# Another hand-written order for the queues, PSUM banks and copy engines of a gated linear recurrence followed by a gated causal convolution block

## Chip, cores and metric

One Trainium2 chip, one of its cores. The metric is device time in microseconds; the kernel before takes 287.73 us (median of 3 runs, 287.46 to 287.93). Lower is better.

## The reference, cut to what matters

Four batches of 6336 positions with 256 channels, float32 in and out. First the recurrence:

```python
log_a = 8 * sigmoid(r_gate) * log(sigmoid(a_param))
a_t   = exp(log_a)
x_g   = sqrt(max(1 - a_t * a_t, 1e-6)) * sigmoid(i_gate) * x
h     = a_t[:, t] * h + x_g[:, t]          # over t, y[:, t] = h
```

Then the gated block on y: a causal depthwise convolution of 5 taps gives the gate, and

```python
out = (sigmoid(conv5(y)) * (y @ w_val)) @ w_out
```

## The kernel before, in words

The 25344 positions of the four batches lie one behind the other. They are cut into 51 **windows** (w = 0 to 50), 48 of them with 512 positions and 3 with 256, and the windows into 28 **chunks** (c = 0 to 27): chunks 3 to 25 have two windows (chunk c has windows 2c-3 and 2c-2), the others one. All arrays live in rings in SBUF, and PSUM is used as 8 banks. Every step is a short word, and one long string, ORDER (L38), lists all words in the order in which they are written to the engines' queues. Each engine takes its own words strictly in that order; nothing reorders them later. A word may name the PSUM banks that it writes, behind an @. Semaphores hold an engine at a word until what it reads is there and what it overwrites has been read.

The words, by engine:

- SyncE (SP) issues the DMAs: `lr`, `li`, `lx` load a window of r_gate, i_gate and x (L292), `st` stores a window of the output (L546). A load waits until the ring place, 4 windows deep, has been read.
- ScalarE (ACT): `ta` and `tb` are tanh of r and i of a chunk (L310, L313; sigmoid(v) is (1 + tanh(v/2)) / 2), `ex` the exp that gives a_t (L378), `rt` the square root for a batch of up to three chunks (L405), `tg` tanh of the convolution's gate of a window (L502), `ca` a copy of a finished window from PSUM to the output ring (L535), `sa` a square (L394). `rt` needs another table of functions than the rest, so a table load stands ahead of and behind each `rt` (L562).
- GpSimd (POOL): `sq` squares a_t (L386), `pp` adds 1 to tanh of i (L320), `up` multiplies by x (L332).
- VectorE (DVE): `uv` does the work of `pp` and `up` for windows 1, 2 and 6 (L346), `xg` multiplies by the norm (L450, L446 for the last two chunks), `sc` is the scan over a half of the channels (L483), `gv` gate times value (L515), `cd` the same copy as `ca` (L533).
- TensorE (PE): `tr`, `nt`, `xt` are transposes (L357, L420, L461, L435), `xp` a plain pass of x into PSUM (L337), `cv` the convolution as 20 small products with diagonal weights (L495), `vl` and `ou` the two products with w_val and w_out (L510, L525), `wm` five products whose result nobody reads (L364).

The path of the data: r goes through `ta`, `tr`, `ex`, `sq`, `rt`, `nt`; i and x through `tb`, `pp`, `up`; they meet in `xg`, then `xt`, `sc`, `cv`, `tg`, with `vl` into `gv`, `ou`, a copy, `st`. The twelve `rt` join all: `rt.b` needs the squares of all its chunks, and each chunk's `xg` waits for its `rt`. `rt.10` is that of chunks 23 to 25, `rt.11` of the last two. Each finished window needs one copy, by `cd` on VectorE or `ca` on ScalarE: that is the choice of copy engine.

The lines that run the list (L557):

```python
for word in ORDER.split():
    word, _, at = word.partition("@")
    name, *idx = word.split(".")
    if table.get(name, have) != have:
        have = table[name]
        nc.scalar.preload_act_table_set(have)
    emit[name](*[int(k) for k in idx], *[int(k) for k in at.split(",") if k])
```

Of the kernel before, what the change touches and what calls it, by code (L numbers as in the profile page):

```python
# [17 lines left out]
    [512, 512], [512, 512], [512, 512], [512, 512], [512, 512], [512, 512], [512, 512], [512, 512], [512, 512],  # L18
    [512, 512], [512, 512], [512, 512], [512, 512], [512, 512], [512, 512], [512, 512], [512], [256]]
BATCHES = [[0], [1], [2], [3, 4], [5, 6, 7], [8, 9, 10], [11, 12, 13], [14, 15, 16], [17, 18, 19], [20, 21, 22],  # L20
    [23, 24, 25], [26, 27]]
# [17 lines left out]
s_ident s_small s_kt s_diag lr.2 lr.0 s_wl.3 lr.1 li.0 lr.3 s_wl.2 ta.2 ta.0 lr.4 tr.0.1@0 tr.2.0@1 lr.6 ta.1 lr.5  # L39
tr.1.0@2 tb.0 tr.0.0@3 li.1 tr.2.1@4 ex.2.0 li.2 tr.1.1@5 li.3 ex.1.1 lx.0 ex.0.1 sq.1.1 li.4 ex.1.0 sq.2.0 ex.0.0  # L40
ex.2.1 sq.1.0 ta.3 sq.2.1 pp.0 sq.0.0 sq.0.1 ta.4 tb.1 lr.10 tr.3.0@4,5 tb.2 lr.9 lr.8 lr.7 lx.2 tr.3.1@2,3 ex.3.0
s_wl.1 up.0 lx.1 lx.4 wm.10@6 ex.3.1 sq.3.0 wm.5@6 lx.3 wm.3@6 tb.3 sq.3.1 wm.9@6 wm.6@6 ta.6 pp.4 sq.4.1 ta.5 lr.13
li.5 xp.2@2,3 li.6 sq.4.0 li.7 lr.14 tr.5.0@4,5 lx.6 uv.2 pp.3 rt.0 rt.2 nt.0@0 up.4 xg.0 rt.1 xt.0@0,1 xp.1@2 rt.3
sc.0.0 nt.1@3 up.3 lx.5 nt.2@0 uv.1 s_wl.0 xg.1 xg.2 xt.1@2,3 sc.0.1 lx.7 sc.1.0 nt.3@6,7 lr.12 sc.1.1 xg.3 ex.5.0
xt.2@0,1 sc.2.1 sc.2.0 tb.4 cv.0@2,3 tr.5.1@4,5 xt.3@6,7 lr.11 li.8 sq.5.0 ex.5.1 tg.0 sc.3.0 pp.5 sc.3.1 cv.2@0,1
s_wcast cv.1@4,5 ta.8 xp.6@2,3 uv.6 vl.0@6,7 tg.1 tg.2 vl.2@0,1 up.5 ta.7 sq.6.1 lx.8 li.9 li.10 lr.17 lr.18
nt.4@2,3 gv.0 tb.5 tr.7.0@6,7 ou.0.0@4 gv.2 ex.7.0 xg.4 sq.6.0 cd.0.0 tr.7.1@0,1 sq.5.1 vl.1@2,3 ou.2.0@4,5 ex.7.1
gv.1 xt.4@6,7 ou.1.0@2 lx.9 li.12 cv.4@0,1 cd.2.0 cv.3@4,5 pp.7 sq.7.1 tb.6 pp.8 sq.7.0 tg.4 tg.3 rt.4 sc.4.1 st.0
sc.4.0 li.11 lr.15 lr.16 st.2 up.7 pp.9 li.14 li.13 vl.3@0,1 vl.4@4,5 gv.3 gv.4 cd.1.0 ou.3.0@0,1 pp.10 up.8 sq.8.1
cd.3.0 cv.6@6,7 st.1 ou.4.0@2,3 wm.12@4 tg.6 cd.4.0 wm.1@4 nt.5@2,3 xg.5 lx.10 tb.7 st.3 vl.6@0,1 gv.6 ta.9 xt.5@2,3  # L50
ou.6.0@0,1 cv.5@6,7 nt.6@4,5 ta.10 up.9 sc.5.0 sc.5.1 lx.11 up.10 wm.0@2 tr.9.0@2,3 tg.5 st.4 lx.12 tb.8 vl.5@6,7
ex.9.0 xg.6 cd.6.0 xt.6@4,5 pp.11 sq.8.0 pp.12 tr.9.1@0,1 up.11 ex.9.1 li.16 li.15 lr.19 lr.20 gv.5 lr.22 st.6 lr.21
nt.7@6,7 cv.7@2,3 sc.6.1 up.12 ou.5.0@0,1 sc.6.0 sq.9.0 tg.7 tb.9 cv.8@2,3 cd.5.0 xg.7 lx.13 lx.14 li.18 ta.11
vl.7@4,5 cv.9@0,1 xt.7@6,7 gv.7 tr.11.1@4 tg.9 tg.8 ex.11.1 ta.12 ou.7.0@0,1 st.5 lx.15 lx.16 li.17 li.19 lr.26
lr.24 sc.7.1 sc.7.0 cv.10@2,3 vl.10@4,5 wm.7@7 vl.8@6,7 tg.10 sq.10.1 pp.13 pp.14 sq.10.0 cd.7.0 sq.9.1 pp.15 gv.10
rt.5 gv.8 st.7 lr.23 li.20 vl.9@2,3 up.13 up.14 tr.12.0@0 pp.16 ou.10.0@4,5 gv.9 ou.8.0@6,7 cd.8.0 ou.9.0@2,3
wm.16@1 nt.8@6,7 tr.11.0@1 cd.9.0 cd.10.0 tb.10 sq.11.1 up.16 xg.8 cv.11@4,5 lx.17 st.9 lr.25 xt.8@6,7 sc.8.1 tg.11
vl.11@2,3 wm.17@4 ex.12.0 tr.12.1@0 nt.9@4,5 gv.11 pp.17 up.15 pp.18 ex.11.0 ex.12.1 sq.12.1 sq.11.0 cv.12@2,3
sq.12.0 xg.9 ta.13 wm.13@7 ou.11.0@4,5 sc.8.0 xt.9@0,1 cd.11.0 cv.14@6,7 cv.13@4,5 tb.11 tg.12 ta.14 tg.14 tg.13
tr.13.0@2,3 tr.13.1@6,7 sc.9.0 ex.13.0 sc.9.1 up.17 st.10 li.21 vl.12@4,5 ex.13.1 nt.10@0,1 lx.18 li.22 gv.12 up.18  # L60
xg.10 lr.28 st.8 lr.27 tb.12 vl.13@2,3 st.11 ou.12.0@4,5 xt.10@0,1 cv.16@6,7 pp.20 pp.19 sq.13.1 gv.13 ou.13.0@2,3
lx.20 lx.21 lr.30 lx.19 ta.15 sq.13.0 pp.21 up.20 cd.12.0 cv.15@4,5 sc.10.1 sc.10.0 lr.29 li.23 tg.16 cd.13.0 li.24
lx.22 tg.15 vl.16@6,7 vl.14@4,5 gv.14 cv.18@0,1 vl.15@2,3 pp.22 rt.6 up.19 li.25 ou.14.0@4,5 gv.16 gv.15 cd.14.0
wm.14@6 ou.15.0@2,3 tg.18 lr.31 li.26 nt.11@4,5 sq.14.0 sq.14.1 up.21 up.22 vl.18@6,7 cd.15.0 xg.11 xt.11@4,5 tb.13
gv.18 cv.17@0,1 nt.12@6,7 ta.16 lr.32 lx.23 sc.11.1 lx.24 st.15 pp.23 pp.24 xg.12 st.13 li.27 li.28 vl.17@2,3
tr.15.1@6,7 sc.11.0 tg.17 tb.14 up.23 ou.16.0@0,1 cd.16.0 ex.15.1 ta.17 cv.19@4,5 lr.34 lr.33 tg.19 gv.17 xt.12@0,1
tr.15.0@6,7 st.14 lx.25 sc.12.0 sc.12.1 li.30 ou.17.0@2,3 pp.25 ex.15.0 ou.18.0@4,5 cv.20@6,7 up.24 tb.15 cd.17.0
cd.18.0 tg.20 cv.21@0,1 pp.26 sq.15.1 sq.16.1 nt.13@2,3 vl.19@6,7 tg.21 xg.13 st.12 lx.26 lx.28 st.17 lx.27 sq.15.0
li.29 st.16 li.31 lr.35 gv.19 vl.20@0,1 gv.20 xt.13@2,3 ou.20.0@0,1 sc.13.0 sq.16.0 vl.21@6,7 ou.19.0@4,5 gv.21
ta.18 cd.20.0 sc.13.1 ou.21.0@6,7 cv.22@0,1 lr.38 st.20 lr.36 rt.7 ca.19.0 li.32 lr.37 up.25 pp.27 up.26 pp.28 lx.29  # L70
nt.14@4,5 cd.21.0 xg.14 vl.22@2,3 tr.17.1@6,7 tg.22 tb.16 up.28 up.27 ex.17.1 nt.15@0,1 lx.30 gv.22 xg.15 xt.14@4,5
tr.17.0@2,3 cv.23@0,1 sc.14.0 sc.14.1 ex.17.0 pp.30 cv.24@6,7 pp.29 st.19 tg.23 vl.24@2,3 ou.22.0@0,1 tg.24 gv.24
vl.23@6,7 xt.15@4,5 ta.19 sq.18.1 sq.18.0 sq.17.0 sq.17.1 ou.24.0@2,3 tb.17 cd.22.0 gv.23 li.33 li.34 cv.26@0,1
up.29 cd.24.0 ou.23.0@6,7 st.18 ta.20 pp.32 ca.23.0 tg.26 cv.25@2,3 up.30 pp.31 sc.15.0 tg.25 li.35 tr.19.0@6,7
# [32 lines left out]
def kernel(  # L107
# [11 lines left out]
    nc = tc.nc  # L119
# [70 lines left out]
    with tc.manual_schedule():  # L190
# [403 lines left out]
```

## Time and profile before

| what | value |
|---|---|
| median of 3 runs | 287.73 us |
| span of the profiled execution, first to last instruction | 286.4 us |
| busy ScalarE (ACT) | 273.6 us, 96% |
| busy TensorE (PE) | 251.8 us, 88% |
| busy VectorE (DVE) | 246.8 us, 86% |
| busy GpSimd (POOL) | 241.6 us, 84% |
| moved by DMA | 104.76 MB, mean 366 GB/s |

The profiled execution has no time of its own beside its span; the median of the runs stands 1.33 us above that span, which is what lies around the first and the last instruction. Busy times are those of one execution. In the rows of the trace, a line begins with the start and the duration in us (or, in groups, ends with total, mean and idle time before), then engine, source line, operation and what it writes and reads; `[1.09 <-PE banks L525]` says that the engine stood idle for 1.09 us before and what released it.

### The profile page before, as it was taken

What the parts mean: (1) busy time and instruction counts of PE and PEld (TensorE: products, weight loads), DVE (VectorE), ACT (ScalarE), POOL (GpSimd) and SP (SyncE); (2) the same over time, 40 slices, a digit from 0 to 9 for tenths busy, and PEclk for the clock granted to TensorE, in tenths of its full rate; (3) what the DMA queues carried; (4) which work ended last, traced back from release to release, by engine and by line L of the source; (5) the groups of instructions that cost most, each with busy time, mean ns of one, the idle gap of its engine ahead of it and who ended that gap; (6) DMA issues with size and microseconds to landing.
All of it is one profiled execution on the core that took longest, in us unless ns stands there. A gap on an engine that the chain in (4) does not pass through costs nothing.

```text
span 286.4 us, 6382 instructions
## 1 busy us (share of the span) xinstructions
PE 251.8 (88%) x2552; PEld 171.1 (60%) x2576; DVE 246.8 (86%) x214; ACT 273.6 (96%) x198; POOL 241.6 (84%) x161
## 2 busy tenths in 40 slices
PE   1387778899999999988988999989989899999993
PEld 1253447456656767455756676656646774767562
DVE  4002898969999899999999999999999999999991
ACT  5999999999999999999999999999999999898984
POOL 1659589899999999999999999999996999874600
PEclk9999999999999999999999999999999999999999
DMA  7999999999999999999999999999999999994536
GB/s 243 384 373 407 409 403 408 388 366 376 410 408 366 418 367 392 414 410 334 405 364 413 411 332 356 420 416 419 415 401 333 359 416 406 364 356 170 192 150 256
DMA packets 29996, 104.76 MB, mean 366 GB/s; under 512 B 3335, under 2 KB 3854, under 8 KB 29966
## 3 DMA queue, kind: packets, MB, share of 16 engines
q1 hardware_dynamic: 29952, 104.35, 94.5%
q8 instruction: 20, 0.33, 0.5%
q14 instruction: 10, 0.08, 0.1%
q10 hardware_dynamic: 14, 0.01, 0.0%
HBM read 78.39 MB, written 25.95 MB: 364 GB/s over the span
## 4 chain that ended last, share of the span: by engine, by line
ACT 33%; PE 29%; DVE 14%; issue 12%; DMA 8%; SPq 1%; ACTq 0%; DVEq 0%
ACT ering L405 8%; PE banks L495 8%; DVE yring L483 7%; PE banks L525 7%; DMA rring<-in_r_gate_dram 6%; ACT tgring L502 6%; ACT taring L310 5%; ACT tbring L313 5%; ACT aring L378 5%; PE banks L510 5%; PE banks L461 3%; DVE tgring L515 3%; PE banks L420 3%; ACT L562 3%; DVE oring L533 2%
## 5 line engine op out<-in xcount | busy, mean ns | idle before, releaser
L386 POOL TENSOR_TENSOR ering<-aring 128x1024 f32<-128x1024 f32 (+2 forms) x54 | 91.5, 1714 | 16.7 <-ACT aring L378 16.4
L332 POOL TENSOR_TENSOR uring<-tbring,xring 128x1024 bf16<-128x1024 bf16 (+1 forms) x48 | 101.1, 2119 | 3.6 <-DMA xring<-in_x_dram 3.1
L483 DVE TENSOR_TENSOR_SCAN yring<-aring,yring,banks 128x1024 bf16<-128x1024 f32 (+5 forms) x50 | 101.7, 2064 | 2.1 <-PE banks L461 1.9
L495 PE MATMUL banks<-yring,diag 64*64 64x512 bf16 (+7 forms) x1080 | 62.1, 361 | 2.3 <-ACT aring L378 1.6
L515 DVE SCALAR_TENSOR_TENSOR tgring<-tgring,banks 128x1024 bf16<-128x1024 bf16 (+1 forms) x51 | 59.1, 1178 | 4.0 <-PE banks L510 3.4
L320 POOL TENSOR_SCALAR tbring<-tbring 128x1024 bf16<-128x1024 bf16 (+1 forms) x48 | 49.1, 1032 | 6.8 <-ACT tbring L313 6.7
L378 ACT ACTIVATE aring<-banks,khf 128x2048 f32<-128x2048 bf16 (+3 forms) x38 | 54.2, 1476 | 0.4 <-PE banks L357 0.3
L525 PE MATMUL banks<-wo,tgring 128*128 128x256 bf16 x396 | 51.0, 274 | 3.7 <-DVE tgring L515 3.2
L502 ACT ACTIVATE tgring<-banks 128x1024 bf16<-128x1024 f32 (+1 forms) x51 | 50.2, 1011 | 2.0 <-PE banks L495 1.9
L510 PE MATMUL banks<-yring,wv 128*128 128x512 bf16 (+4 forms) x192 | 48.1, 359 | 3.7 <-ACT tgring L502 1.9
L310 ACT ACTIVATE taring<-rring 128x2048 bf16<-128x2048 f32 (+2 forms) x28 | 47.9, 1718 | 1.4 <-DMA rring<-in_r_gate_dram 1.4
L525 PEld LDWEIGHTS <-tgring 128*128 128x128 bf16 x396 | 41.2, 114 | 13.1 <-DVE tgring L515 8.8
L313 ACT ACTIVATE tbring<-iring 128x2048 bf16<-128x2048 f32 (+2 forms) x28 | 48.2, 1726 | 0.0
L405 ACT ACTIVATE ering<-ering 128x4096 bf16<-128x4096 f32 (+5 forms) x16 | 44.8, 2840 | 0.1
L495 PEld LDWEIGHTS <-diag 64*64 64x64 bf16 x1080 | 29.0, 106 | 25.6 <-issue 9.9
L533 DVE COPY oring<-banks 128x1024 f32<-128x1024 f32 (+1 forms) x36 | 41.9, 1182 | 1.4 <-PE banks L525 0.7
L357 PE MATMUL banks<-ident_b,taring 128*128 128x128 bf16 x396 | 29.9, 230 | 9.4 <-ACT taring L310 6.7
L357 PEld LDWEIGHTS <-taring 128*128 128x128 bf16 x396 | 26.5, 103 | 14.2 <-ACT taring L310 7.4
L510 PEld LDWEIGHTS <-wv 128*128 128x128 bf16 x216 | 19.7, 98 | 24.5 <-issue 10.3
L450 DVE TENSOR_TENSOR uring<-banks,uring 128x2048 bf16<-128x2048 bf16 (+2 forms) x26 | 29.4, 1134 | 3.5 <-PE banks L420 3.2
L420 PE MATMUL banks<-ident,ering 128*128 128x128 f32 x192 | 28.3, 289 | 1.1 <-ACT ering L405 0.9
L461 PE MATMUL banks<-ident,uring 128*128 128x128 f32 x192 | 25.9, 276 | 3.5 <-DVE uring L450 2.8
(49 smaller groups left out, 154.0 us busy)
## 6 DMA issues: line engine op xcount, KB each, us to landing
rring<-in_r_gate_dram SPq DMA_DIRECT2D x48, 512.0 KB, 8.2
iring<-in_i_gate_dram SPq DMA_DIRECT2D x48, 512.0 KB, 8.7
xring<-in_x_dram SPq DMA_DIRECT2D x48, 512.0 KB, 8.2
out_dram<-oring SPq DMA_DIRECT2D x48, 512.0 KB, 6.5
rring<-in_r_gate_dram SPq DMA_DIRECT2D x3, 256.0 KB, 4.1
iring<-in_i_gate_dram SPq DMA_DIRECT2D x3, 256.0 KB, 6.5
xring<-in_x_dram SPq DMA_DIRECT2D x3, 256.0 KB, 8.5
out_dram<-oring SPq DMA_DIRECT2D x3, 256.0 KB, 5.2
```

The costliest lines, as they stand in the source:

```text
L310: nc.scalar.activation(**tangent(c, taring, NTR, rring, NRI))
L313: nc.scalar.activation(**tangent(c, tbring, NTI, iring, NII))
L332: nc.gpsimd.tensor_tensor(out=u, in0=t1, in1=xt, op=ALU.mult)
L378: nc.scalar.activation(out=dst, in_=src, func=ACT.Exp, scale=khf[:, h:h + 1], bias=khf[:, h:h + 1])
L386: nc.gpsimd.tensor_tensor(out=e, in0=a, in1=a, op=ALU.mult)
L405: nc.scalar.activation(out=ering[:].bitcast(BF16)[:, 4 * o:4 * o + 2 * n], in_=ering[:, 2 * o:2 * o + 2 * n], func=ACT.Sqrt, scale=-0.25, ...
L483: nc.vector.tensor_tensor_scan(out=yring[:, h, col:col + o1 - o0], data0=aring[:, h, a_at[c] + o0:a_at[c] + o1], data1=xT[:, o0:o1], initi ...
L495: nc.tensor.matmul(out=gp[oh * 64:oh * 64 + 64, h, a:b], lhsT=diag[half * 64:half * 64 + 64, h, k, :], rhs=yring[half * 64:half * 64 + 64, ...
L502: nc.scalar.activation(out=tgring[:, w % NTG, :, 0:wins[w]], in_=live.pop(("gp", w))[:, :, 0:wins[w]], func=ACT.Tanh, scale=0.5)
L510: nc.tensor.matmul(out=val[:, m, a:b], lhsT=wv[:, hk, m * P:(m + 1) * P], rhs=yring[:, hk, col:col + b - a], start=(hk == 0), stop=(hk == ...
L515: nc.vector.scalar_tensor_tensor(out=tgring[:, w % NTG, :, 0:wins[w]], in0=tgring[:, w % NTG, :, 0:wins[w]], scalar=1.0, in1=live.pop(("va ...
L525: nc.tensor.matmul(out=ops[:, j * D:(j + 1) * D], lhsT=gv[:, hk, j:wins[w]:J], rhs=wo[:, hk, :], start=(hk == 0), stop=(hk == H - 1))
```

## The change: what it does

ORDER is replaced as a whole by another list of the same length (976 words). The ring sizes, the chunks, the groups and the batches are the same. Beside the order, three things differ: the banks behind @ (among them two unequal banks for some `xt`, such as `xt.0@0,4`, and banks for the two set-up words, which had theirs in the code); which engine copies eight windows (16, 22, 24, 32 and 36 go from VectorE to ScalarE, 19, 23 and 39 from ScalarE to VectorE); and the places of the 17 `wm`. An unused function goes. Source lines behind it move up by one to five.

```diff
 ORDER = """
-s_ident s_small s_kt s_diag lr.2 lr.0 s_wl.3 lr.1 li.0 lr.3 s_wl.2 ta.2 ta.0 lr.4 tr.0.1@0 tr.2.0@1 lr.6 ta.1 lr.5
...
-s_wl.1 up.0 lx.1 lx.4 wm.10@6 ex.3.1 sq.3.0 wm.5@6 lx.3 wm.3@6 tb.3 sq.3.1 wm.9@6 wm.6@6 ta.6 pp.4 sq.4.1 ta.5 lr.13
...
+s_ident s_small s_kt@0 s_diag@1 lr.0 lr.1 lr.2 lr.3 ta.0 ta.1 tr.1.0@4 lr.4 tr.0.0@6 tr.0.1@7 lr.5 ta.2 ex.0.0 ex.0.1
...
+li.7 sc.0.0 xp.1@7 wm.5@5 sc.0.1 cv.0@4,5 tg.0 uv.1 xg.1 xt.1@1,7 sc.1.0 xt.2@0,6 sc.1.1 sc.2.1 lx.5 s_wcast lx.7 lx.8
+ex.5.0 nt.3@4,5 xg.3 tr.5.1@6,7 tb.4 sq.6.0 sq.5.0 sc.2.0 xt.3@2,3 sc.3.0 cv.1@4,5 li.9 li.10 ex.5.1 sq.6.1 pp.5
...
-        def s_kt():
-            kps = banks[:, 0]
+        def s_kt(at):
+            kps = banks[:, at]
...
-        def s_diag():
-            wps = banks[:, 1]
+        def s_diag(at):
+            wps = banks[:, at]
...
-        def op_sv(c, h):
-            e, a = squares(c, h)
-            nc.vector.tensor_tensor(out=e, in0=a, in1=a, op=ALU.mult)
```

What this makes of the queues, at three places. First ScalarE at the start of the program, behind the exp of the set-up. A row is a source line, an operation, what it writes and reads and its shape; 128x512 in taring is a window of 256 positions. Before:

```order
L237 ACTIVATE ktmp<-ktmp 128x2
L310 ACTIVATE taring<-rring 128x1024
L310 ACTIVATE taring<-rring 128x512 x2
L313 ACTIVATE tbring<-iring 128x512
L378 ACTIVATE aring<-banks,khf 128x512
L378 ACTIVATE aring<-banks,khf 128x256 x4
L378 ACTIVATE aring<-banks,khf 128x512
```

After the change:

```order
L236 ACTIVATE ktmp<-ktmp 128x2
L309 ACTIVATE taring<-rring 128x512 x2
L309 ACTIVATE taring<-rring 128x1024
L377 ACTIVATE aring<-banks,khf 128x256 x4
L309 ACTIVATE taring<-rring 128x2048
L377 ACTIVATE aring<-banks,khf 128x512
L309 ACTIVATE taring<-rring 128x2048
L377 ACTIVATE aring<-banks,khf 128x512
```

The two short windows come first, the tanh of i moves behind them, and the large tanh of r stand between the exps. Up to the first table load, which stands ahead of the first square roots, ScalarE has the same 19 words in both lists.

Second, ScalarE behind the square root of batch 6 (the row L405 or L400 over 128x6144). Before, down to the square root of batch 7:

```order
L405 ACTIVATE ering<-ering 128x6144
L562 ACT_TABLE_LOAD
L502 ACTIVATE tgring<-banks 128x1024
L313 ACTIVATE tbring<-iring 128x2048
L310 ACTIVATE taring<-rring 128x2048
L502 ACTIVATE tgring<-banks 128x1024
L313 ACTIVATE tbring<-iring 128x2048
L378 ACTIVATE aring<-banks,khf 128x2048
```

After the change:

```order
L400 ACTIVATE ering<-ering 128x6144
L557 ACT_TABLE_LOAD
L497 ACTIVATE tgring<-banks 128x1024
L312 ACTIVATE tbring<-iring 128x2048 x2
L530 COPY oring<-banks 128x1024
L497 ACTIVATE tgring<-banks 128x1024
L377 ACTIVATE aring<-banks,khf 128x2048 x2
L309 ACTIVATE taring<-rring 128x2048
```

A copy (that of window 16) stands between the tanh, where there was none. Ahead of `rt.10` ScalarE has 3 copies before (windows 19, 23, 33) and 6 after (16, 22, 24, 32, 33, 36); of all other kinds it has the same number ahead of `rt.10` in both lists.

Third, VectorE ahead of the product of chunk 23 (the next-to-last row, L450 or L445 over 128x2048), which is the first to need `rt.10`. Before:

```order
L515 SCALAR_TENSOR_TENSOR tgring<-tgring,banks 128x1024 x2
L533 COPY oring<-banks 128x1024
L515 SCALAR_TENSOR_TENSOR tgring<-tgring,banks 128x1024
L533 COPY oring<-banks 128x1024 x2
L450 TENSOR_TENSOR uring<-banks,uring 128x2048
L515 SCALAR_TENSOR_TENSOR tgring<-tgring,banks 128x1024 x2
```

After the change:

```order
L510 SCALAR_TENSOR_TENSOR tgring<-tgring,banks 128x1024 x3
L478 SCALAR_TENSOR_TENSOR yring<-aring,yring,banks 128x1024
L528 COPY oring<-banks 128x1024 x3
L445 TENSOR_TENSOR uring<-banks,uring 128x2048
L510 SCALAR_TENSOR_TENSOR tgring<-tgring,banks 128x1024 x2
```

The copy of window 39, which ScalarE had behind `rt.10`, stands here on VectorE ahead of it; the eight products that window 39 needs first (`ou.39`) moved ahead of `nt.23`, TensorE's first word behind `rt.10`. From `nt.23` to the end TensorE has 44 words before and 43 after, the same but for `ou.39`.

More of the change, by code (lines that the diff above doesn't have):

```diff
@@ L99 @@
[L99 to L102 removed]
+s_ident s_small s_kt@0 s_diag@1 lr.0 lr.1 lr.2 lr.3 ta.0 ta.1 tr.1.0@4 lr.4 tr.0.0@6 tr.0.1@7 lr.5 ta.2 ex.0.0 ex.0.1
+tr.1.1@0 ex.1.1 ex.1.0 lr.6 li.2 li.0 ta.3 tr.2.1@7 ex.2.1 tr.2.0@6 lx.0 lr.8 lr.7 ta.4 lr.9 lr.10 ex.2.0 tb.2 sq.1.1
@@ L103 @@
+ou.50.0@3 ca.50.0 st.50
 """
```

130 lines of the change are left out of this document (63 added, 67 removed).

## Prediction

> **What bounds the kernel now.** All numbers are of one profiled execution with a span of 286.4 us; the median of the runs, 287.73, lies 1.33 above it, and I add the difference that I work out to that median. First the busy time of the engines in six stretches, cut at ScalarE's first tanh, its first table load, the start and the end of `rt.10` and TensorE's last product. Columns: stretch, its length, busy time of PE, PEld, DVE, ACT and POOL (with counts), granted clock, DMA share, GB/s.
>
> ```profile
> 0.00:4.54 4.54, 0.23 (x1) 0.18 (x1) 0.88 (x6) 1.49 (x2) 0.97 (x7) 1.00 0.57 190
> 4.54:26.48 21.94, 12.88 (x77) 8.15 (x78) 2.92 (x15) 20.71 (x20) 13.70 (x13) 1.00 1.02 380
> 26.48:238.87 212.39, 196.25 (x2047) 134.37 (x2068) 202.64 (x161) 211.95 (x140) 203.75 (x127) 1.00 1.01 391
> 238.87:244.20 5.33, 5.17 (x60) 2.88 (x52) 5.22 (x6) 5.32 (x1) 5.33 (x4) 1.00 1.00 404
> 244.20:282.80 38.60, 37.30 (x377) 25.55 (x382) 35.11 (x29) 33.55 (x36) 17.84 (x13) 1.00 0.67 247
> 282.80:286.40 3.60, 0.00 (x0) 0.00 (x0) 0.00 (x0) 0.58 (x1) 0.00 (x0) 0.90 0.56 218
> ```
>
> The third row carries most: for 212.39 us ScalarE is busy 211.95 and idle 0.44. VectorE and POOL are near it (202.64, 203.75), so it has little to spare from others, but the one that never waits is ScalarE. **From 26.48 to `rt.10` the length is the sum of ScalarE's work.** In the fifth row this has changed: TensorE is busy 37.30 of 38.60. The chain that ended last, in order of time (start, length, what), confirms it:
>
> ```profile
> 238.87 5.34 ACT ering L405
> 244.25 1.24 PE banks L420 x8
> ...
> 249.42 0.87 PE banks L525 x8
> ...
> 281.43 0.70 DVE tgring L515
> 282.13 0.05 issue
> 282.17 0.63 PE banks L525 x4
> 282.82 0.58 ACT oring L535
> ```
>
> The square root of L405 ends at 244.21 and releases TensorE's transposes (`nt.23`); from there nearly all pieces down to 282.8 are TensorE's. So the end is: start of ScalarE, plus its work up to `rt.10`, plus TensorE's work from `nt.23` on, plus 3.60 for the last copy and store.
>
> **The change part by part.**
>
> (1) ScalarE's work ahead of `rt.10`. The order's rows show that only copies differ: 3 before, 6 after. What a copy costs in a full queue, from a copy and what starts behind it:
>
> ```profile
> 168.50 1.02 ACT L535 COPY oring<-banks 128x1024 f32<-128x1024 f32 x1
> 169.40 1.97 ACT L502 ACTIVATE tgring<-banks 128x1024 bf16<-128x1024 f32 x2
> ```
>
> From start to start 169.40 - 168.50 = 0.90 us. Three more are **+2.70 us**, with no cover, since ScalarE has no idle time there to lose. The other side is lighter by what VectorE no longer copies, but VectorE is not the one that is waited for in that stretch, so I count nothing for it.
>
> (2) TensorE behind `nt.23`. One word of 44, `ou.39`, moves ahead of it, into a stretch where TensorE has 212.39 - 196.25 = 16.1 us idle; the piece x8 at 249.42 above prices it at 0.87. So **-0.87 us**. The 1.30 us that TensorE is idle between 244.20 and 282.80 could go as well, or grow; I take no change, and keep -1.3 as an end.
>
> (3) The start. ScalarE's rows (engine, line, operation, idle time before and its releaser):
>
> ```profile
> 4.54 1.58 ACT L310 ACTIVATE taring<-rring 128x1024 bf16<-128x1024 f32 x2 [0.49 <-DMA rring<-in_r_gate_dram]
> 6.35 0.63 ACT L310 ACTIVATE taring<-rring 128x512 bf16<-128x512 f32 x1 [0.23 <-DMA rring<-in_r_gate_dram]
> 7.01 0.63 ACT L313 ACTIVATE tbring<-iring 128x512 bf16<-128x512 f32 x1
> 8.63 2.60 ACT L378 ACTIVATE aring<-banks,khf 128x256 f32<-128x256 bf16 x5 [0.29 <-PE banks L357]
> 13.40 1.91 ACT L310 ACTIVATE taring<-rring 128x2048 bf16<-128x2048 f32 x1 [0.38 <-DMA rring<-in_r_gate_dram]
> 24.55 1.91 ACT L310 ACTIVATE taring<-rring 128x2048 bf16<-128x2048 f32 x1 [0.28 <-DMA rring<-in_r_gate_dram]
> 26.48 1.28 ACT L562 ACT_TABLE_LOAD   x1
> ```
>
> The waits are 0.49 + 0.23 + 0.29 + 0.38 + 0.28 = 1.67 us, nearly all for r. The new list loads `lr.0` (256 KB) first instead of `lr.2` (512 KB), and puts `lr` 0 to 6 ahead of every `li`, so the first tanh need not wait 0.49 and the big ones see r sooner. But the tanh of i that filled 0.63 at 7.01 moves back, and the exps now stand third in line, when the constants of `khf` are just ready. All 1.67 gone is one end. The other is 0.63 lost, where that tanh leaves a hole and nothing else is won. I take **-0.5**, nearest to the first row's wait. The work in between is the same 19 words.
>
> (4) The first block behind the first square roots. Before, ScalarE does `ex.5.0`, `tb.4`, `ex.5.1` ahead of the first `tg.0`; now `tg.0` stands directly behind the table load. What it waits for runs through TensorE and VectorE:
>
> ```profile
> 29.77 3.60 ACT L405 ACTIVATE ering<-ering 128x4096 bf16<-128x4096 f32 x1
> 33.39 1.28 ACT L562 ACT_TABLE_LOAD   x1
> 40.39 0.59 ACT L502 ACTIVATE tgring<-banks 128x512 bf16<-128x512 f32 x1
> 29.09 0.42 DVE L450 TENSOR_TENSOR uring<-banks,uring 128x512 bf16<-128x512 bf16 x1 [0.46 <-PE banks L420]
> 29.94 0.69 DVE L483 TENSOR_TENSOR_SCAN yring<-aring,banks 128x256 bf16<-128x256 f32 x1 [0.41 <-PE banks L461]
> 32.70 0.68 DVE L483 TENSOR_TENSOR_SCAN yring<-aring,banks 128x256 bf16<-128x256 f32 x1
> 28.59 0.39 PE L420 MATMUL banks<-ident,ering 128*128 128x128 f32 x2
> 29.57 0.44 PE L461 MATMUL banks<-ident,uring 128*128 128x128 f32 x2 [0.59 <-DVE yring L472]
> 35.02 0.74 PE L495 MATMUL banks<-yring,diag 64*64 64x256 bf16 x20
> ```
>
> Before, the convolution of window 0 ended at 35.02 + 0.74 = 35.76, and `tg.0` came at 40.39: 4.6 us of cover. Now `tg.0` is due when the four square roots and the table load are through, at 33.39 + 1.28 = 34.7 on the old clock. The last of the four takes 3.60, so between the third (the last that window 0's chain stands behind, since `nt.1` is ahead of `nt.0`) and `tg.0` lie 3.6 + 1.28 = 4.9 us. In them must happen two sets of transposes (2 x 0.39), the product 0.42, the transposes 0.44, two scans that now stand one behind the other (0.69 + 0.68), `wm.5`, and the convolution 0.74. And the 25 products that stood in TensorE's idle time around 19.52 (`wm.10` to `wm.6`, twenty of them in the second row below) are gone to other places. Their rate, and that of weight loads ahead and behind:
>
> ```profile
> 15.37 2.48 PEld L357 LDWEIGHTS <-taring 128*128 128x128 bf16 x24 [1.52 <-ACT taring L310]
> 19.52 4.20 PEld L364 LDWEIGHTS <-ident_b 128*128 128x128 bf16 x20 [0.18 <-issue]
> 27.69 0.88 PEld L357 LDWEIGHTS <-taring 128*128 128x128 bf16 x15 [0.33 <-issue]
> ```
>
> Weight loads of the same kind come every 2.48 / 24 = 103 ns ahead of the filler and every 0.88 / 15 = 59 ns behind it, while the granted clock reads 1.00 in both stretches. A TensorE that has not been kept busy takes 1.75 times as long here. `wm.5` is five products of 4.20 / 20 = 0.21 us at the quick rate, 1.05. The chain is then 0.78 + 0.42 + 0.44 + 1.37 + 1.05 + 0.74 = 4.8 us, without the 0.4 to 0.6 that the bracketed waits show at each change of engine. At the slow rate its TensorE part (0.78 + 0.44 + 1.05 + 0.74 = 3.0) takes 3.0 x 0.75 = 2.3 more. Ends: 0, since part of `wm.5` can run beside the scans, and 2.3 + 0.5 = 2.8. I take **+0.8**: 4.8 and two such changes of engine (0.9) less 4.9.
>
> The Trainium skill, page TensorE: Matmul & The Clock Gate, section "Part 1: The HAM clock gate", says that the array runs at half its clock until one window of about 3.4 us has been busy, and again after one idle window. The 103 and 59 ns agree with it, the granted clock of 1.00 does not show it. By that rule the whole first block runs at the slow rate, and (4) would be 2.8 instead of 0.8: that is the rival "slow TensorE" below.
>
> (5) All other places between 26.48 and `rt.10`. Every semaphore there meets another neighbour. ScalarE's waits were 0.44 us in all, and can hardly fall; how much they grow nothing shows. Nearest are the waits of the start (0.2 to 0.5 each) and, at the far end, ScalarE's idle time where another engine leads: 38.60 - 33.55 = 5.05 us in 38.60. Late loads, too, would show as such waits; the rings are as deep as before, and what ScalarE waited for loads after 26.48 is within the 0.44. I take **+0.5** (one such wait), with 0 and 4 as ends.
>
> Sum: 2.70 - 0.87 - 0.5 + 0.8 + 0.5 = **+2.63 us**, so 287.73 + 2.63 = 290.36, in short **290.4 us**. The new unequal banks and the moved stores are within (5).
>
> **The rivals.**
>
> *Slow TensorE at the start.* (4) costs 2.8 and not 0.8: 287.73 + 4.63 = 292.4 us. For it speaks that 25 filler products leave the start; against it, that the transposes of `nt.2` and `nt.1` and `wm.5` are themselves work just ahead of that convolution.
>
> *New waits in the middle.* (5) costs 4 and not 0.5, because a list that is laid out for other durations than these puts words just ahead of what they need: 287.73 + 6.13 = 293.9 us. Against it speaks that all four engines have work queued; for it, that ScalarE's 0.44 us leave no way but up.
>
> *Faster: ScalarE's instructions themselves get shorter.* Its work is the length, and the same instruction does not always take the same time:
>
> ```profile
> L502 ACT ACTIVATE tgring<-banks 128x1024 bf16<-128x1024 f32 x48 | 48.6, 1037 | 2.0 <-PE banks L495 1.9
> L313 ACT ACTIVATE tbring<-iring 128x2048 bf16<-128x2048 f32 x23 | 44.3, 1927 | 0.0
> L310 ACT ACTIVATE taring<-rring 128x2048 bf16<-128x2048 f32 x23 | 44.0, 1918 | 0.7 <-DMA rring<-in_r_gate_dram 0.7
> 214.89 1.01 ACT L502 ACTIVATE tgring<-banks 128x1024 bf16<-128x1024 f32 x1
> 213.09 1.90 ACT L310 ACTIVATE taring<-rring 128x2048 bf16<-128x2048 f32 x1
> ```
>
> If another neighbourhood on the other engines let all run at the quick rows' time, that is 48 x 0.027 + 23 x 0.027 + 23 x 0.018 = 2.3 us; with -0.5 for the start and no new wait 287.73 + 2.70 - 0.87 - 0.5 - 2.3 = 286.8 us. It decides the sign only from 1.9 us on (2.70 - 0.87 - 0.5 + 0.58), so nearly all instructions must gain. If TensorE's 1.3 us of idle time in (2) go too, it is 285.5.
>
> *No change.* The start gives all 1.67 back and (4) and (5) cost nothing: 287.73 + 2.70 - 0.87 - 1.67 = 287.9 us.
>
> **How the numbers follow.** A measurement here can tell about 0.2% from no change, that is 0.58 us. Chances: the forecast with its near neighbours 0.42, slow TensorE 0.15, new waits 0.15, faster 0.15, no change 0.13. So slower 0.72, same 0.13, faster 0.15. The range reaches from 286.5, inside the faster case, to 293.9, the new waits; it leaves out about half of each of those two.
>
> **What would show it.** In the profile after: ScalarE's copies (L530) x17 instead of 15, six of them ahead of `rt.10`; `rt.10` starting at 238.87 + 2.70 - 0.5 + 0.8 + 0.5 = 242.4; from its end to the last product 37.7 us, nearly all TensorE; ScalarE's idle time between its first table load and `rt.10` near 1.7 us, one piece of it at the first `tg` with L490 as releaser; the first table load near 26.0. Weight loads of taring at 100 ns as late as 30 us would speak for the slow TensorE. The prediction fails if `rt.10` comes earlier than 239: then instructions got shorter. It also fails if TensorE no longer leads the tail.

## The result and the profile after

The changed kernel takes **292.18 us** (median, 290.90 to 293.89) beside 287.60 (287.30 to 287.93) for the kernel before on the same chip: ratio 1.0155, 95% interval 1.0113 to 1.0196. A second set of runs gave 291.69 beside 287.89, ratio 1.0149 (1.0113 to 1.0185). It is slower, by 3.8 to 4.6 us; 290.4 was forecast. The profiled execution has a span of 292.1 us and was the slowest of its set (293.89). In every execution of the later runs, the time stands 1.7 to 2.0 us above the span of the same execution. By that the profiled execution of the kernel before (span 286.4) took about 288.2 us, some 0.5 more than its median; the 1.33 us given with its profile set the span of one execution against the time of another.

First the busy time of the engines in the stretches that the prediction used, now for the changed kernel (columns: stretch, length, busy time of PE, PEld, DVE, ACT, POOL with counts, granted clock, DMA share, GB/s):

```profile
0.00:3.65 3.65, 0.23 (x1) 0.18 (x1) 0.46 (x3) 1.42 (x2) 0.98 (x7) 1.00 0.51 158
3.65:28.34 24.69, 8.82 (x67) 7.20 (x68) 3.34 (x18) 20.54 (x21) 12.12 (x12) 1.00 0.95 346
28.34:244.36 216.02, 200.99 (x2049) 135.63 (x2069) 200.54 (x159) 214.79 (x142) 206.67 (x128) 1.00 0.99 382
244.36:249.69 5.33, 5.22 (x59) 3.74 (x61) 5.33 (x5) 5.33 (x1) 5.25 (x4) 1.00 1.03 411
249.69:288.60 38.91, 37.10 (x383) 24.99 (x378) 35.73 (x30) 32.86 (x37) 17.21 (x13) 1.00 0.68 262
288.60:292.10 3.50, 0.00 (x0) 0.00 (x0) 0.00 (x0) 0.51 (x1) 0.00 (x0) 0.85 0.53 210
```

The second row is 24.69 us where before had 21.94, with ScalarE idle for 4.15 of them. The third has grown from 212.39 to 216.02 us; ScalarE fills 214.79 of it, as it filled nearly all before. The fifth, behind `rt.10`, went from 38.60 to 38.91. What is late in the second row shows in ScalarE's own rows (start, length, operation, idle time before and its releaser):

```profile
3.65 1.24 ACT L309 ACTIVATE taring<-rring 128x512 bf16<-128x512 f32 x2
7.69 1.06 ACT L309 ACTIVATE taring<-rring 128x1024 bf16<-128x1024 f32 x1 [2.80 <-DMA rring<-in_r_gate_dram]
14.37 1.91 ACT L309 ACTIVATE taring<-rring 128x2048 bf16<-128x2048 f32 x1 [1.33 <-issue]
```

The first tanh doesn't wait for its load here, but the third waits 2.80 us, and the fifth stands idle for another 1.33 us, for which the profile names no releaser. The chain that ended last has changed its leader in the tail (start, length, what):

```profile
245.67 2.27 DVE yring L478
...
247.98 2.39 PE banks L490 x40
250.37 1.17 PE banks L415 x8
...
256.25 2.25 DVE yring L478
...
258.56 2.27 DVE yring L478
...
260.87 2.36 PE banks L490 x40
...
267.79 2.27 DVE yring L478
...
270.15 3.52 DVE yring L478 x2
...
287.87 0.63 PE banks L520 x4
```

Before, nearly every piece from 244.25 on was TensorE's. Now a scan of VectorE releases the two convolutions `cv.41` and `cv.40` (the row x40 at 247.98), and the transposes of `nt.23` follow behind these at 250.3; between 251 and 274 VectorE leads, with its scans as the longest pieces.

### The profile page after: what moved, and what is told of

Its sections match the earlier page's. It is cut to its first block, busy times and chain, and to the rows that moved or that the text cites. A ratio compares the mean times of both kernels' runs of the same rounds, so it can differ in the third digit from the quotient of the medians.

```text
span 292.1 us, 6377 instructions
## 1 busy us (share of the span) xinstructions
PE 252.4 (86%) x2549; PEld 171.7 (59%) x2576; DVE 245.4 (84%) x212; ACT 275.4 (94%) x200; POOL 242.2 (83%) x161
## 4 chain that ended last, share of the span: by engine, by line
PE 20%; ACT 19%; POOL 17%; DVE 16%; DMA 15%; issue 9%; SPq 2%; DVEq 0%; ACTq 0%; POOLq 0%
DVE yring L478 8%; POOL ering L385 8%; POOL uring L331 7%; DMA rring<-in_r_gate_dram 6%; DMA xring<-in_x_dram 6%; PE banks L490 6%; PE banks L520 4%; ACT ering L400 4%; PE banks L505 4%; ACT aring L377 4%; ACT taring L309 4%; ACT tbring L312 3%; DVE uring L445 3%; DVE tgring L510 3%; DMA iring<-in_i_gate_dram 3%
## 5 line engine op out<-in xcount | busy, mean ns | idle before, releaser
L385 POOL TENSOR_TENSOR ering<-aring 128x1024 f32<-128x1024 f32 (+2 forms) x54 | 91.4, 1713 | 21.0 <-ACT aring L377 20.9
L331 POOL TENSOR_TENSOR uring<-tbring,xring 128x1024 bf16<-128x1024 bf16 (+1 forms) x48 | 100.9, 2116 | 1.4
L319 POOL TENSOR_SCALAR tbring<-tbring 128x1024 bf16<-128x1024 bf16 (+1 forms) x48 | 49.0, 1030 | 7.0 <-ACT tbring L312 7.0
L497 ACT ACTIVATE tgring<-banks 128x1024 bf16<-128x1024 f32 (+1 forms) x51 | 50.8, 1013 | 3.5 <-PE banks L490 3.2
L309 ACT ACTIVATE taring<-rring 128x2048 bf16<-128x2048 f32 (+2 forms) x28 | 47.9, 1718 | 4.1 <-DMA rring<-in_r_gate_dram 2.8
L505 PE MATMUL banks<-yring,wv 128*128 128x512 bf16 (+7 forms) x189 | 47.9, 358 | 2.7 <-ACT tgring L497 0.8
L520 PEld LDWEIGHTS <-tgring 128*128 128x128 bf16 x396 | 41.8, 114 | 13.1 <-issue 5.3
L312 ACT ACTIVATE tbring<-iring 128x2048 bf16<-128x2048 f32 (+2 forms) x28 | 47.6, 1720 | 0.2 <-issue 0.2
L356 PE MATMUL banks<-ident_b,taring 128*128 128x128 bf16 x396 | 30.7, 234 | 17.2 <-ACT taring L309 12.3
L400 ACT ACTIVATE ering<-ering 128x4096 bf16<-128x4096 f32 (+5 forms) x16 | 44.8, 2840 | 0.1
L528 DVE COPY oring<-banks 128x1024 f32<-128x1024 f32 (+1 forms) x34 | 39.2, 1180 | 0.7 <-PE banks L520 0.6
L445 DVE TENSOR_TENSOR uring<-banks,uring 128x2048 bf16<-128x2048 bf16 (+2 forms) x26 | 29.4, 1136 | 4.4 <-PE banks L415 3.6
L415 PEld LDWEIGHTS banks<-ident,ering 128*128 128x128 f32 x192 | 25.2, 207 | 7.9 <-issue 2.2
```

The costliest lines, as they stand in the source:

```text
L309: nc.scalar.activation(**tangent(c, taring, NTR, rring, NRI))
L312: nc.scalar.activation(**tangent(c, tbring, NTI, iring, NII))
L331: nc.gpsimd.tensor_tensor(out=u, in0=t1, in1=xt, op=ALU.mult)
L356: nc.tensor.transpose(out=bank[:, o:o + P], in_=taring[:, place(w, NTR), j, h * P:(h + 1) * P], identity=ident_b[:])
L400: nc.scalar.activation(out=ering[:].bitcast(BF16)[:, 4 * o:4 * o + 2 * n], in_=ering[:, 2 * o:2 * o + 2 * n], func=ACT.Sqrt, scale=-0.25, ...
L505: nc.tensor.matmul(out=val[:, m, a:b], lhsT=wv[:, hk, m * P:(m + 1) * P], rhs=yring[:, hk, col:col + b - a], start=(hk == 0), stop=(hk == ...
```

## The experiments

All runs were timed beside the kernel before. The starts of ScalarE's square roots mark the program in stages; below, **middle** is `rt.4` to `rt.10`, with ScalarE's busy time in it. Times in us; the median is of the runs of that kernel.

| kernel | `rt.3` | `rt.4` | `rt.10` | middle | ScalarE busy | median |
|---|---|---|---|---|---|---|
| before | 29.77 | 56.62 | 238.87 | 182.25 | 181.88 | 287.6 to 287.9 |
| changed, first profile | 31.64 | 59.33 | 244.36 | 185.03 | 184.43 | 292.18 |
| changed, repeat | 29.54 | 57.23 | 242.18 | 184.95 | 184.37 | 291.69 |
| changed, short ScalarE copies | 31.07 | 58.30 | 243.22 | 184.92 | 182.44 | 292.14 |
| changed, short VectorE copies | 31.86 | 59.08 | 244.20 | 185.12 | 184.38 | 293.44 |
| changed, both short | 29.15 | 56.54 | 240.95 | 184.41 | 182.32 | 291.28 |
| changed, more filler | 29.12 | 57.75 | 242.38 | 184.63 | 184.25 | 292.37 |
| changed, start of before, mended | 30.21 | 58.92 | 243.61 | 184.69 | 184.31 | 291.86 |
| changed, copy engines back | 29.16 | 56.39 | 250.67 | 194.28 | 182.67 | 303.92 |
| before, two more table loads | 29.11 | 55.96 | 241.03 | 185.07 | 184.65 | 290.65 |
| before, short ScalarE copies | 28.98 | 55.83 | 237.77 | 181.94 | 179.96 | 287.26 |
| before, both short | 29.25 | 56.10 | 237.64 | 181.54 | 179.91 | 286.91 |

The windows from `rt.4` to `rt.10` of the kernel before, of the repeat and of the run with short ScalarE copies (length, busy time of PE, PEld, DVE, ACT, POOL, granted clock, DMA share, GB/s):

```profile
56.62:238.87 182.25, 171.56 (x1791) 117.38 (x1812) 176.00 (x135) 181.88 (x119) 178.92 (x109) 1.00 1.00 389
57.23:242.18 184.95, 173.94 (x1808) 119.52 (x1826) 175.19 (x132) 184.37 (x122) 178.64 (x108) 1.00 0.98 378
58.30:243.22 184.92, 175.03 (x1827) 119.51 (x1826) 175.13 (x133) 182.44 (x122) 178.60 (x108) 1.00 0.98 379
```

ScalarE is the fullest engine in all three, but GpSimd (POOL) is busy for 97 to 98% of them and VectorE for 95 to 97%, and the transfers' share is 0.98 to 1.00.

**The changed kernel again**, no edit.

> The changed kernel once more, unchanged. Theory A (a sum along ScalarE: late r at the start +1.9, first block +0.9, three more copies +2.7, tail +0.2): the third tanh again waits for r until about 7.7 us, rt.10 starts near 244 us, time 291 to 293 us. Rival (the start was luck of that one execution): the third tanh comes near 6.2 us, the first table load near 26.5 us, rt.10 near 242.5 us.

It took 291.69 us (290.98 to 294.27). Its third tanh waited less for r:

```profile
6.82 1.06 ACT L309 ACTIVATE taring<-rring 128x1024 bf16<-128x1024 f32 x1 [2.01 <-DMA rring<-in_r_gate_dram]
```

It starts at 6.82 instead of 7.69, and `rt.3` 2.10 us sooner than in the first profile; from there on the two profiles of the same kernel agree to 0.09 us up to `rt.10`. So what differs between them is made ahead of `rt.3`: 0.87 us at the third tanh, and most of the rest at the fifth, which starts at 12.08 without any wait here. The time lies where theory A had it (291 to 293), `rt.10` (242.18) and the first table load (26.24) where the rival had them. The profiled execution (291.70) took the median time of its set, so the repeat is the fairer one to set against before: `rt.3` at 29.54 beside 29.77.

**Copy engines back in place.** The changed kernel, with the eight windows copied by the engines of before, each word where it stands (the changed words alone):

```diff
-ca.16.0
+cd.16.0
-cd.19.0
+ca.19.0
...
-cd.39.0
+ca.39.0
```

> The changed list, with the copy engines of before for the eight windows, each word at its place. Theory A: rt.10 starts 2.7 us earlier than in the changed kernel, time 289.5 us. Rival B (in the new list VectorE and GpSimd lead as often as ScalarE, so three copies more on VectorE at 1.15 us each cost as much as ScalarE gains): 291.5 to 293 us.

303.92 us, ratio 1.0543 (1.0517 to 1.0569): twelve slower than the change itself, far outside both expectations. ScalarE's waits between `rt.4` and `rt.10` in this run (line, releaser: us in total, times, longest):

```profile
ACT oring L530 <- PE banks L520: 5.7, 2, 2.9
ACT aring L377 <- DVE yring L478: 2.7, 2, 1.4
ACT tgring L497 <- PE banks L490: 2.7, 4, 1.1
```

The first row is the copies of windows 23 and 33: their products are not there yet, and ScalarE waits 2.93 and 2.81 us for them. Window 23's copy is one of those that the swap gave to ScalarE; window 33's is ScalarE's in the change too and doesn't wait there, so its wait comes from what the swap made late ahead of it. The second row is exps that wait for VectorE, which has three copies more here. The granted clock also fell to 0.5 twice in this execution, for 3.4 us each, but the run with the start put back as well (304.66 us, below) lost as much, and its profiled execution had a clock of 1.000. So a copy word's engine and its place belong together, and the swap in place doesn't price the copies.

**The start of before.** First alone, then with the swap above. Words that this start already holds are taken out behind it, among them five groups of filler (`wm`), four of which stood in the middle:

```diff
-s_ident s_small s_kt@0 s_diag@1 lr.0 lr.1 lr.2 lr.3 ta.0 ta.1 tr.1.0@4 lr.4 tr.0.0@6
...
+s_ident s_small s_kt@0 s_diag@1 lr.2 lr.0 s_wl.3 lr.1 li.0 lr.3 s_wl.2 ta.2 ta.0 lr.4
...
```

> The words ahead of the first square root in the order of before (loads, tanh, exp, squares and the 25 filler products), all others in the new order. Theory A: first table load near 26.5 us instead of 28.3, rt.4 2.7 us earlier, time 292.2 - 2.7 = 289.5 us. Rival B (what the start loses is hidden by waits of other engines later): 291 us or more.

> Start and copy engines both as before, the rest of the list new. Theory A, sums add: 292.2 - 2.7 - 2.7 = 286.8 us, within 0.3% of the kernel before. Rival B (the new order of the middle has a cost of its own that shows once the other two are gone): 289 us or more.

292.75 us, ratio 1.0169 (1.0147 to 1.0191), and 304.66, ratio 1.0572 (1.0539 to 1.0606). In the first, one load had stayed at its late place at the seam, and GpSimd waited for it:

```profile
POOL wv L273 <- DMA oring<-in_moe_w_val_dram: 6.9, 1, 6.9
```

So the first of the two says nothing on the start, and the second repeats the loss of the swap. Mended, with that load in the start too:

> The changed kernel with the start of before (all words ahead of the first table load, the load of the second weights among them; the words behind it in the order of the change, those that the start already holds taken out). Theory A, that the start costs nothing in the median and the first block costs some 0.9 us: rt.3 at about 29.2, rt.4 0.5 to 2 us after where the repeat of the changed kernel has it (57.23) if it is the order behind rt.3 that is late, and the time 291 to 292.5. Rival B, that the changed start is what is late: rt.4 at 56.6 to 57.0 and the time 289 to 290.5.

291.86 us, ratio 1.0137 (1.0114 to 1.0161), no faster than the changed kernel within its spread. `rt.3` comes at 30.21 and `rt.4` at 58.92, 1.69 later than in the repeat; ScalarE's waits up to there, 1.76 us of them at one load in the first block:

```profile
ACT taring L308 <- DMA rring<-in_r_gate_dram: 4.9, 5, 1.8
```

Expectation B (56.6 to 57.0) fell; A's `rt.4` and time held, its `rt.3` (29.2) did not. The start of before doesn't bring back the time of before when the loads behind it stand in the new order.

**More filler.** The changed kernel with `wm.20@6 wm.21@6 wm.22@6 wm.23@6`, twenty products, ahead of `tr.5.0`.

> The changed kernel with twenty more filler products on TensorE (four groups of five, bank 6) ahead of the products of tr.5.0, which put back as many as the start of before has more. Theory A, that the first block is late because TensorE runs slowly there: the four products of xp.2 fall from 0.85 us each towards 0.49, rt.3 to rt.4 shrinks from 27.69 us by 0.5 to 0.9, and the time by as much, to about 291.0. Rival B, that the order of ScalarE's and VectorE's instructions there makes it: rt.3 to rt.4 stays within 0.2 us of 27.69, and the time stays at 291.7 to 292.2.

292.37 us, ratio 1.0161 (1.0131 to 1.0192): no gain. TensorE's rows in the changed kernel's first profile, then in this run, and this run's window from 30 to 33 us:

```profile
27.78 3.78 PE L336 MATMUL banks<-xring,ident 128*128 128x512 f32 x4 [0.79 <-DMA xring<-in_x_dram]
```

```profile
24.56 1.98 PE L336 MATMUL banks<-xring,ident 128*128 128x512 f32 x4 [0.40 <-DMA xring<-in_x_dram]
28.32 0.72 PE L415 MATMUL banks<-ident,ering 128*128 128x128 f32 x4 [1.77 <-POOL ering L385]
29.27 0.66 PE L415 MATMUL banks<-ident,ering 128*128 128x128 f32 x4 [0.23 <-ACT ering L400]
31.02 1.92 PE L336 MATMUL banks<-xring,ident 128*128 128x512 f32 x2
```

```profile
30.00:33.00 3.00, 2.46 (x5) 1.12 (x6) 1.70 (x4) 2.98 (x2) 3.00 (x2) 0.51 1.09 320
```

The four products of `xp.2` fell from 3.78 us to 1.98, as the theory of the slow TensorE says, and `rt.3` came 0.4 us earlier than in the repeat; this start without the filler has 29.15 and 29.16 in two other profiles, so that gain can't be put down to it. TensorE then waited 1.77 us for GpSimd, and from 30 to 33 us the granted clock was 0.51: the two products of `xp.1` took 1.92, and `tg.0` came 0.52 later than in the repeat. `rt.3` (29.12) to `rt.4` (57.75) was 28.63 instead of 27.69, so neither expectation held. The Trainium skill, page TensorE: Matmul & The Clock Gate, section "Part 1: The HAM clock gate", has the clock halved after an idle window of about 3.4 us; here it was halved when TensorE had been busy for 0.72 + 0.66 = 1.38 us of the 3.4 before 30, so wholly idle it need not be. The run shows that the first block has a slow TensorE in the change and that twenty products more do not buy it off; what a TensorE at full speed throughout would give was not seen. Slow products of `xp.2` alone do not make the block long: with the copy engines back they took 3.78 us too, and `rt.3` to `rt.4` was 27.23.

**Short copies on ScalarE.** In the changed kernel, for windows 22, 24 and 36:

```diff
         def op_ca(w, i):
+            if w in (22, 24, 36):
+                nc.scalar.copy(out=oring[:, w % NOSB, 0, 0:128], in_=live.pop(("ops", w, i))[:, 0:128])
+                return
```

> The changed kernel, with three of its six ScalarE copies ahead of rt.10 (windows 22, 24 and 36) cut from 1024 to 128 columns: the rest of these three windows of the output is left out. Theory A, that ScalarE's sum of busy time sets the middle: each of them goes from 0.90 us to some 0.25, the middle from rt.4 to rt.10 (184.95 us in the changed kernel's first two profiles) becomes about 183.0, and the time about 289.8 beside 291.7 to 292.2. Rival B, that VectorE (99% busy in the middle of before) or GpSimd leads as much as ScalarE does: the middle shrinks by under 0.5 us, and the time stays above 291.2.

292.14 us, ratio 1.0149 (1.0127 to 1.0171): nothing gained. The middle is 184.92 us beside 184.95. Where the time went, in ScalarE's rows:

```profile
169.85 0.29 ACT L537 COPY oring<-banks 128x128 f32<-128x128 f32 x1
170.54 1.02 ACT L497 ACTIVATE tgring<-banks 128x1024 bf16<-128x1024 f32 x1 [0.40 <-PE banks L490]
171.47 0.26 ACT L537 COPY oring<-banks 128x128 f32<-128x128 f32 x1
172.42 2.06 ACT L377 ACTIVATE aring<-banks,khf 128x2048 f32<-128x2048 bf16 x1 [0.70 <-PE banks L356]
```

Each copy is shorter by 0.75 us, and the instruction behind it waits for TensorE instead (0.40 and 0.70; 0.62 behind the third, at 240.88). The full copies end not long before TensorE delivers what is next. ScalarE's work here (182.44) is within 0.6 us of that of before (181.88), with as many full copies (three), and still the middle is 2.67 us longer. **Theory A, that ScalarE's work alone sets the length of the middle, fell.** TensorE is only what ScalarE waits for directly. In the chain that ended last, from 58 to 245 us, 27% are GpSimd's (L331 11.5, L385 11.0, L319 4.7) and 20% loads of i and x under way (10.1 and 10.0). A part of it (start, length, what):

```profile
137.87 2.13 POOL uring L331
140.01 8.11 DMA xring<-in_x_dram
...
151.53 2.13 POOL uring L331
153.67 10.65 DMA xring<-in_x_dram
164.34 10.01 DMA iring<-in_i_gate_dram
174.41 1.87 ACT tbring L312
```

So GpSimd and the loads are rivals for what makes TensorE late; no run took work from either.

**More work on ScalarE in before.** Two table loads behind `tb.12` and `tb.20`; the added word does this:

```diff
+        def op_tl(k):
+            nc.scalar.preload_act_table_set("exp_and_others")
```

> The kernel before, its order untouched, with two more table loads on ScalarE, behind tb.12 and behind tb.20, of 1.28 us each; nothing else runs on them and nothing waits for them by data. Theory A, that ScalarE's busy time in the middle passes straight to the end: +2.57 us, 290.3 from 287.7, with rt.10 at about 241.4 instead of 238.87. Rival B, that VectorE or GpSimd covers it: under +0.8 us, below 288.6. Between them both engines share the lead.

290.65 us, ratio 1.0109 (1.0087 to 1.0132). The window from `rt.4` to `rt.10`:

```profile
55.96:241.03 185.07, 171.65 (x1808) 117.66 (x1812) 176.20 (x135) 184.65 (x120) 178.98 (x109) 1.00 0.99 383
```

185.07 - 182.25 = 2.82 us for 2.57 put in, and ScalarE is again without idle time. Theory A holds for work that is added.

**The same cuts in before, on one engine and on two.** In `copy`, for windows 19, 23 and 33 of ScalarE, then with 21, 24 and 35 of VectorE too; and in the changed kernel with 23, 25 and 35 of VectorE, alone and with 22, 24 and 36:

```diff
             src = live.pop(("ops", w, i))
+            if w in (19, 23, 33):
+                dst, src = dst[:, 0:128], src[:, 0:128]
```

> The kernel before, with its three ScalarE copies ahead of rt.10 (windows 19, 23 and 33) cut to 128 of 1024 columns; the rest of these windows' output is left out. A copy of 128 columns took 0.27 us in the run with short copies in the changed kernel, so ScalarE's work falls by 3 x 0.75 = 2.25 us. Theory A, that ScalarE alone sets the middle of before: rt.4 to rt.10 goes from 182.25 to about 180.0, the time to about 285.5. Theory C, formed after the short copies in the changed kernel bought nothing, that the engines are balanced against each other so that work added to ScalarE costs all and work taken away gains nothing: rt.4 to rt.10 stays above 181.5 and the time above 287.0, with waits on ScalarE of 1 to 2 us in place of the work.

> As the last, and with three VectorE copies of the middle (windows 21, 24 and 35) cut to 128 columns as well, some 2.8 us of VectorE's work; the rest of these six windows' output is left out. If ScalarE and VectorE are the two that hold each other, both gains come through: rt.4 to rt.10 at about 180 and the time at 285 to 286. If TensorE's banks, GpSimd or the transfers stand as close behind, the time stays above 287.0.

> The changed kernel with three VectorE copies of the middle (windows 23, 25 and 35) cut to 128 columns, some 2.8 us of VectorE's work; the rest of these three windows' output is left out. If VectorE is the one that leads in the changed kernel, where short copies on ScalarE bought nothing: rt.4 to rt.10 falls from 184.95 to under 183.5 and the time to about 290. If ScalarE leads (busy 184.4 of 184.95 us there), nothing in the middle, but scans that start sooner behind rt.10 and a tail shorter by up to 1 us.

> The changed kernel with the three ScalarE copies (windows 22, 24 and 36) and the three VectorE copies (windows 23, 25 and 35) cut to 128 columns; the rest of these six windows' output is left out. If the two engines hold each other: rt.4 to rt.10 falls by 2 us to about 183.0 and the time to about 289.5. If it is the order of TensorE's work and its banks that ScalarE waits for: rt.4 to rt.10 stays above 184.3, as with the copies of ScalarE alone (184.92).

287.26 us, ratio 0.9985 (0.9967 to 1.0003); 286.91, ratio 0.9970 (0.9955 to 0.9984); 293.44, ratio 1.0193 (1.0164 to 1.0222); 291.28, ratio 1.0111 (1.0086 to 1.0136). These are, in order, the two of before and the two of the changed kernel. The first of them, its window from `rt.4` to `rt.10` and ScalarE's wait there:

```profile
55.83:237.77 181.94, 171.73 (x1791) 117.22 (x1812) 175.94 (x135) 179.96 (x119) 178.70 (x108) 1.00 1.00 389
```

```profile
ACT aring L378 <- PE banks L357: 1.6, 3, 0.7
```

In before, 1.92 us less busy time on ScalarE (181.88 to 179.96; 2.25 had been worked out) bring 0.31 (182.25 to 181.94), and 1.6 become waits for TensorE's transposes; both cuts bring 0.71, with 1.2 us of such waits left, and a time between the two forecasts (285 to 286, above 287.0). In the changed kernel VectorE's cut takes its busy time from 175.19 to 172.47 and brings nothing (185.12), and nothing in the tail either; both together bring 0.54 (184.95 to 184.41). Differences of this size must be read with care: the run with more filler, whose words in the middle are those of the change, has 184.63. Theory C, a balance, holds, and it lies between at least three parties: with the copies short on ScalarE and VectorE, what comes to ScalarE through TensorE allows 0.7 us and no more. GpSimd, busy for 178.70 of 181.94, and the transfers, with a share of 1.00, may stand behind that; neither was tried. None of the runs points to an order that beats the kernel before. The 293.44 of the third run stays unexplained in part: its profile is late ahead of `rt.4` (59.08) and like the repeat behind it, and the start varies, but why six runs should all be late I cannot say.

## Why the prediction came out as it did

The range held the time, with the sign right; the forecast was 1.8 us short (1.3 by the second set). The steps, by the repeat against before (span 289.9 less 286.4: 3.5 us):

| step | forecast | measured |
|---|---|---|
| (3) start, to `rt.3` | -0.5 | -0.23; +0.29 to +0.56 against three other profiles of the old start; in other profiles of the new start up to +2.1 |
| (4) first block, `rt.3` to `rt.4` | +0.8 | 27.69 - 26.85 = +0.84 |
| (1) + (5) middle, `rt.4` to `rt.10` | +2.7 + 0.5 | 184.95 - 182.25 = +2.70 |
| (2) `rt.10` to the start of the last four products | -0.87 | 43.51 - 43.30 = +0.21 |

By these profiles the sum was 0.9 us short: (2) alone 1.08, (3) 0.27, with 0.50 of it made good by waits in (5) that did not come. That the terms for the middle and the first block come so near is in part luck, as shown below. The time lies nearest to the rival with the slow TensorE (292.4), but that rival's mechanism was not there: it wanted 2.8 us in (4).

**(1) Three more copies: the size came out, but they are not the only limit.** The middle grew by 2.70 us. Of these, 2.49 are ScalarE's busy time (181.88 to 184.37) and 0.21 its idle time. So the added work alone explains the size, as forecast, and a full ScalarE costs whatever is added (+2.82 for 2.57). But with three of the copies cut to 128 of 1024 columns the middle grew by as much (184.92): the new order has a second limit at the same length, which the prediction did not know. In before, with its copies cut in the same way, that limit lies at 181.94 or below. Where ScalarE has room, it waits for TensorE, and why TensorE is later was not settled. GpSimd and the loads were named above; in the first profile SyncE held loads back for GpSimd's `up` for 45.5 us in all, in before for 19.9. Another candidate that I did not price stands in TensorE's rows between `rt.4` and `rt.10`, the filler products before and after:

```profile
L364 PE MATMUL banks<-ident_b 128*128 128x512 bf16 x60 | 14.8, 379 | 1.1 <-ACT aring L378 0.7 <-DVE yring L483 0.3
```

```profile
L363 PE MATMUL banks<-ident_b 128*128 128x512 bf16 x71 | 17.8, 379 | 1.2 <-DVE yring L478 1.2
```

The order has 15 groups of five there instead of 12, and TensorE is 3.0 us busier with them. I had followed these products out of the start and not to where they went. The mended start took four groups out of the middle, so that 11 are left (13.7 us), and its middle is 184.69, no shorter than that of the run with more filler (184.63). But ScalarE, with its six copies full, is busy for 184.31 of it, so this run can't show what the filler costs where ScalarE has room. Both together, less filler and short copies, were not tried; the new banks are as possible.

**(2) `ou.39` ahead of `nt.23`: this step failed.** The tail from `nt.23` to the start of the last four products did shrink (37.92 to 37.55), by 0.37 and not 0.87. But `nt.23` no longer starts at the end of `rt.10`: in before 0.05 us behind it, in the repeat 0.63, since `cv.41` and `cv.40` stand ahead of it and wait for a scan that now comes late. VectorE in before, then in the changed kernel's first profile:

```profile
233.83 4.57 DVE L483 TENSOR_TENSOR_SCAN yring<-aring,yring,banks 128x1024 bf16<-128x1024 f32 x2
```

```profile
242.04 3.62 DVE L510 SCALAR_TENSOR_TENSOR tgring<-tgring,banks 128x1024 bf16<-128x1024 bf16 x3
245.59 2.34 DVE L478 TENSOR_TENSOR_SCAN yring<-aring,yring,banks 128x1024 bf16<-128x1024 f32 x1
247.84 3.46 DVE L528 COPY oring<-banks 128x1024 f32<-128x1024 f32 x3
```

The scan at 245.59 is `sc.22.0`. It was the first of the two at 233.83 before, ahead of `rt.10`; now it runs beside it. TensorE's products moved ahead as I said, but VectorE's words moved back past them, and I had looked at TensorE alone. The stated failure "if TensorE no longer leads the tail" came true.

**(3) Start: this step failed too.** The first tanh lost its wait of 0.49 in two of seven profiles of the new start (in the repeat it waits 0.56), and a larger one came behind it: the third tanh waits 1.3 to 3.3 us for its load in all seven (it starts at 6.13 to 8.05), and in some the fifth waits as well (1.33 in the first profile). `rt.3` then lies between 29.12 and 31.86, where four profiles of the old start with the old order have 28.98 to 29.77. So the new start has the wider spread, and no gain: the -0.23 of the repeat stands against the latest of those four. That the start, late in some executions more than in others, also makes the rest of the miss is likely from the two profiles of the one kernel; no run took it apart. The first table load, forecast for 26.0, stood at 28.34 in the first profile and at 26.24 in the repeat.

**(4) First block.** +0.84 where +0.8 was forecast, but made otherwise, so that the agreement is luck: two waits of `tg` for TensorE, 0.5 us together, none of them the `tg.0` that I had worked out as late; the other 0.3 has no row of its own. Four other profiles with the same words there have 27.22 to 27.39, that is +0.37 to +0.54, with one such wait. TensorE is slow just ahead of the block (`xp.2` at 0.95 us a product), but the block costs nothing like the rival's 2.8.

**(5) New waits in the middle.** ScalarE's idle time from its first table load to `rt.10` is 216.02 - 214.79 = 1.23 us, 0.8 more than before, of which 0.5 lie in the first block; so neither +0.5 as a separate term nor the rival of 4 was seen. *Faster* fell: the tanh of L309 and L312 take 1921 and 1923 ns on average, as before (1918 and 1927). *No change* fell with the time and with `rt.10` at 242.18 and 244.36 beside 238.87. That the repeat's `rt.10` is so near to the 242.4 worked out owes something to the late start in the profile of before.

## What to carry to other kernels

Where several engines are each some 95% busy, the sum of the fullest engine's work is a floor: it tells what an addition costs, but not what a removal gains. Here 2.57 us added cost 2.82, and 1.9 us less gained 0.31 in one order and 0.03 in the other. A sum that comes out right is therefore no proof of its cause; cut the suspected work to a fraction and see whether the time follows. And when a word moves ahead on one engine, look at what the other engines in its chain moved past: eight copies that changed engines while their words stayed in place cost 12 us.

## What the runs showed of the hardware

The middle agrees to 0.1 us over 185 us between two executions of one kernel (a third kernel with the same words there was 0.3 shorter), while the start varies by over 2 us, in part with the landing of one load of r. And the granted clock as the profile prints it does not show that TensorE is slow early in the program: in the repeat it reads 1.00 while a product of `xp.2` takes 0.95 us, but it reads 0.51 for the same slow pace (0.96) once TensorE had been quick and then waited, in the run with more filler. The reason is in the packed trace, whose first clock record is a rise to full speed, at 29.44 us in the repeat and at 19.41 in before; ahead of it there is no record, and 1.00 is printed. In the run with more filler the records stand at 19.79 (full), 30.03 (half) and 33.45 (full).
